# Attention mixed with a token MLP on one core: an eviction moved from ScalarE to VectorE, the start of a unit's maximum held back before some stretches, and one output store issued later

## The chip, the cores and the metric

The kernel runs on one core of a Trainium2 chip. The metric is the device time of one execution in microseconds (us); lower is better. The time before is the median of three runs, 1621.32 us (1620.71 to 1622.15). The core has five engines that are named here as the profile names them: PE is TensorE (PEld its weight loads), DVE is VectorE, ACT is ScalarE, POOL is GpSimd, and SP is the engine that issues nearly all DMAs. Each engine takes its instructions in the order in which the program lists them.

## The reference

The input is `x` with 2048 tokens of 640 channels. Two branches are computed from it and mixed with a gate of its own for each token. Branch A is attention with 32 query heads of 20 channels over one shared key head and one shared value head; branch B is an MLP across the tokens.

```python
g = _sigmoid((x * gate_w).sum(-1, keepdims=True))
# branch A
q = (x @ wq).reshape(B, S, H, Dh).transpose(0, 2, 1, 3)      # H = 32, Dh = 20
k, v = x @ wk, x @ wv                                        # one head for all queries
p = _softmax(jnp.einsum("bhqd,bkd->bhqk", q, k) * (Dh ** -0.5), axis=-1)
a = jnp.einsum("bhqk,bkd->bhqd", p, v).transpose(0, 2, 1, 3).reshape(B, S, H * Dh) @ wo
# branch B
h = _layernorm(x, axis=-1)
u = _gelu(jnp.einsum("bsd,sf->bdf", h, w1) + b1)             # F = 1728
b = jnp.einsum("bdf,fs->bds", u, w2) + b2                    # then transposed to (B, S, D)
return g * a + (1 - g) * b
```

## The kernel before, in words

**Units.** Attention is cut into 32 units: a unit is four heads by 512 queries. A unit needs three kinds of matrix work on PE. *Maxima*: scores of 128 queries by 512 keys are written to a bank of PSUM (`ms_next`, L506) and VectorE takes the maximum along the keys (L514, tile `mp`); 64 such tiles make a unit. The 64 partial maxima are put together by one VectorE reduction (`ms_done`, L536), three small POOL instructions (L532 to L534), a VectorE transpose (`store_max`, L541), a DMA to DRAM (`m_scr`, L542) and four DMAs that bring them back as two rows of the query tile (`fetch_max`, L549), so that the maximum is subtracted inside the score product itself. *Scores*: transposed scores of 128 keys by 512 queries (`qk`, L689), on which ScalarE computes the exponential (L701, tile `p`). *Values*: `p` times `v` (`pv_mm`, L722), four heads at once, which also sums the softmax denominators.

**Stretches and bursts.** The main loop runs 244 stretches, numbered `j`. `arrange` interleaves in one stretch eight score tiles, four to ten maxima tiles and some products of other work (`fs`) on the two row halves of PE, which run beside each other. After each stretch comes a burst: sixteen L722 matmuls (two key blocks of one unit). Its result is copied out by ScalarE (`collect`, L740 or L743) and added up by POOL (L744). The other work comes in three stages: products with W1 (L1012, 24 in each half and stretch), products with W2 (L837, 20, 20, 20 and then 21), and in the last 44 stretches the output projection of 11 token tiles (L961, 15 in each half and stretch). After the loop come 12 tail stretches (`stretch(i)`) with the remaining projections (L910), and then the end of the last unit.

**The planner.** Which instruction stands where is decided while the program is built: `begins`, `issue`, `spend` and `next_free` keep estimated clocks for the two PE lanes, for `dve` and `act`, and for each PSUM bank (`free`), and the next free bank and the next lane are taken by these clocks. On the chip each engine just follows its list and waits on semaphores. `end` in `arrange` is the list of functions that close a piece of other work; they are called when the last product of a stretch has been listed, right behind `signal()`, a tiny VectorE memset (`flag`, L711) that waits for that product and lets the other row half go on.

**The projection's end.** One projection (one token tile, half the channels) takes two stretches and accumulates in the bank `g`. `a_jobs.done` closes it. Before, the list `spare` holds False for the whole loop, so the else branch is always taken in it: ScalarE scales the sums by the gate (L972), POOL adds the MLP's part `yt` (L973). The store of the tile (L975) is appended to `stores` and issued a stretch later.

**The last maxima.** Unit 31's maxima are finished inside tail stretch 2; `m_scr` is written and fetched at its end, and tail stretch 4 is the first whose scores need them. The first tail projection (`jobs[0]`, token tile 11, tile `parts[st]`) is finished by VectorE (L922) in the same stretch 2, and its store (L926) is issued where it is finished, in front of the write of `m_scr` on SP's list.

Of the kernel before, what the change touches and what calls it, by code (L numbers as in the profile page):

```python
# [10 lines left out]
F32 = mybir.dt.float32  # L11
# [7 lines left out]
P = 128  # L19
# [20 lines left out]
def mix_kernel(ctx: ExitStack, tc: tile.TileContext, A_x, A_wq, A_wk, A_wv, A_wo,  # L40
# [635 lines left out]

    units = [(n, kb) for n in range(NU) for kb in range(NS)]
    ptiles = {}
    spare = [False]
    last = {"half": None, "ins": None, "sig": None}  # L680
    flag = const.tile([1, 1], F32, name="flag")

# [182 lines left out]
        nc.sync.dma_start(out=yt, in_=y_scr[st * P:(st + 1) * P, :])  # L865

    parts = {}
    tail = [[], []]
    loaded = []
    CUT = 3 * P  # L870
# [24 lines left out]
    def tail_job(n):  # L895
        st, r0, r1 = jobs[n]
        oT, yt = room(n)
        acc, at, ready = {}, {}, []

        def mm(c, k, d, h, first, last):  # L900
            if first:
                i = at[d, h] = busy[h] = next_free()
                while any(k == i for _, k, _ in reduces):
                    reduces.pop(0)[2]()
                acc[d, h] = bank(i)
                free[i] = float("inf")
            o, w = ((oT[:, 0], wo_hi), (oT[:, 1], wo_hi), (oT[:, 0], wo_lo))[k]
            r = slice(64 * h, min(r1 - c * P, 64 * h + 64))
            region = [("x", at[d, h])]
            touch(nc.tensor.matmul(acc[d, h][:, :HD2], o[r, c, :], w[r, c, d * HD2:(d + 1) * HD2],  # L910
                                   start=first, stop=last), writes=region)
            if last:
                ends = lane[h] + 0.15
                while reduces and reduces[0][0] < ends:
                    reduces.pop(0)[2]()
                free[at[d, h]] = spend("dve", 0.48, ends) + 0.24
                sl = slice(d * HD2, (d + 1) * HD2)
                if st not in parts:
                    parts[st] = fin.tile([P, D], F32, name="yo") if r1 == D else spare_row(st)
                add = parts[st] if d in ready or r0 else yt  # L920
                ready.append(d)
                touch(nc.vector.scalar_tensor_tensor(parts[st][:, sl], acc[d, h][:, :HD2], g_col[:, st:st + 1],  # L922
                                                     add[:, sl], op0=ALU.mult, op1=ALU.add), region)
                if len(ready) == 4:
                    if r1 - r0 == D:
                        nc.sync.dma_start(out=y_out[st * P:(st + 1) * P, :], in_=parts[st])  # L926
# [16 lines left out]
    def a_jobs(st):  # L943
        hold = {}

        def load():
            oT, yt = oTs[st % 2], yts[st % 2]
            load_a(st, D, oT, yt)
            hold["o"], hold["y"] = oT, yt
            hold["a"] = fin.tile([P, D], F32, name="yo")  # L950

        total = 6 * DC

        def mm(c, k, d, half):
            if not hold.get("n"):
                hold["p"], hold["n"] = ps_g.tile([P, NB], F32, name="g"), 0
            oT = hold["o"]
            o, w = ((oT[:, 0], wo_hi), (oT[:, 1], wo_hi), (oT[:, 0], wo_lo))[k]
            hold["n"] += 1
            r = slice(64 * half, 64 * half + 64)  # L960
            other_tile(half, nc.tensor.matmul(hold["p"][:, :HD2], o[r, c, :], w[r, c, d * HD2:(d + 1) * HD2],  # L961
                             start=(hold["n"] == 1), stop=(hold["n"] == total)))

        def done(d):
            sl = slice(d * HD2, (d + 1) * HD2)
            at, yt = hold["a"], hold["y"]
            hold["n"] = 0
            if spare[0]:
                nc.vector.scalar_tensor_tensor(at[:, sl], hold["p"][:, :HD2], g_col[:, st:st + 1], yt[:, sl],
                                               op0=ALU.mult, op1=ALU.add)  # L970
            else:
                nc.scalar.activation(at[:, sl], hold["p"][:, :HD2], AF.Copy, scale=g_col[:, st:st + 1])  # L972
                nc.gpsimd.tensor_add(at[:, sl], at[:, sl], yt[:, sl])  # L973
# [183 lines left out]
    def arrange(h, ss, own, other, fs, end):  # L1157
        ss, own, other, fs = list(ss), list(own), list(other), list(fs)
        n_s, n_m, n_f = len(ss), len(own), len(fs)
        lx, lf = layout(n_s, n_m, n_f, len(other))  # L1160
        pairs.clear()
        at = lx.replace("m", "").find("S")
        if at >= 0:
            pairs.update({at: 0, at + 1: 2})
        lx = [(k, (own if k == "m" else ss).pop(0)) for k in lx]
        lf = [(k, (other if k == "m" else fs).pop(0)) for k in lf]
        lanes = [None, None]
        lanes[h], lanes[1 - h] = lx, lf
        left = n_f
        while lanes[0] or lanes[1]:  # L1170
            k = min((k for k in range(2) if lanes[k]), key=lambda k: begins(k, lanes[k][0][0]))
            kind, f = lanes[k].pop(0)
            issue(k, kind, f)
            left -= kind == "f"
            if kind == "f" and not left:
                seen = lane[k] + 0.3
                while reduces and reduces[0][0] < seen:
                    reduces.pop(0)[2]()
                signal()
                spend("dve", 0.01)  # L1180
                state["f"] = seen + 0.6
                for f in end:
                    f()
                    state["f"] = max(state["f"], spend("act", 0.4, lane[k] + 0.2) + 0.1)
        while reduces:
            reduces.pop(0)[2]()

# [37 lines left out]
    for j in range(n_st):  # L1225
# [22 lines left out]
            f()  # L1248
        if follow:
            follow.pop(0)()  # L1250
        if not follow:
            n = len(row_max)
            follow += ms_done()
            if follow:
                follow.pop(0)()
                follow.append(lambda n=n: store_max(n))
# [19 lines left out]
    free.append(state["f"])  # L1276
    free[o_bank] = float("inf")
    o_last = {}
    spare[0] = True

    def visits(us):
        for u in us:
# [57 lines left out]
    def stretch(i):  # L1340
        u0 = 2 * n_st + 2 * i
        lanes, tiles = [None, None], [None, None]
        state["f"] = 0.0
        for b in range(2):
            block = []
            ss = [("s", lambda at, u=u, pr=pr, b=b, block=block: qk(u, pr, b, at, block))
                  for u in (u0, u0 + 1) for pr in range(2)]
            ms = [("m", ms_next(b)) for _ in range((3, 3, 2)[i] if i < 3 else 0)]
            lanes[b] = tail_take(b, math.ceil(len(tail[b]) / (TAIL // 2 - i)))
            tiles[b] = ms + ss if i == 2 else [x for n in range(4) for x in ss[n:n + 1] + ms[n:n + 1]]  # L1350
        for k in best_order(tiles, lanes, i):
            issue(k % 2, *(tiles, lanes)[k // 2][k % 2].pop(0))
        while reduces:
            reduces.pop(0)[2]()
        while stores:
            stores.pop(0)()
        if i == 2:
            for f in ms_done():
                f()
            store_max(NU - 1)  # L1360
            stores.pop()()
            fetch_max(NU - 1)
        settle()
# [12 lines left out]
    def next_acc():  # L1376
# [1 line left out]
        free[i] = max(free) + 1.0  # L1378
        return i

    assert not tail[0] and not tail[1] and not any(later)
    pool = pools["last"]
    whole = (pool.tile([P, NB // 32, 32], F32, name="ot"), pool.tile([P, NB // 32], F32, name="rl"),
             copies.tile([P, NB], F32, name="part"), *(pools["q5"][:, i, :] for i in range(2)))
    turn = [last_half(k, o_last[NU - 1], whole) for k in range(2)]
    for f in turn[0][:5] + turn[1][:2] + turn[0][5:] + turn[1][2:5]:
        f()
    accs = {}
# [73 lines left out]
```

## Time and profile before

| what | value |
|---|---|
| median of three runs | 1621.32 us |
| the profiled execution | 1621.41 us, of which the span from first to last instruction is 1619.6 us |
| busy, share of the span | PE 99%, VectorE 85%, ScalarE 78%, POOL 53% |
| instructions | 39588 |
| granted clock of TensorE | 1.00 |
| chain that ended last | PE 97% |
| L972, ScalarE, scale of a projection | 22 times, mean 612 ns |
| L973, POOL, its addition | 22 times, mean 878 ns |

The span and the execution's own time differ by 1.8 us, which lies around the instructions. A busy time in the profile runs from an instruction's start to its end; instructions of ScalarE and VectorE overlap by a part of that, so how fast they follow one another is read from the distance of their starts. PE counts as busy nearly throughout, even where its instructions wait for a bank, so a stretch is measured here from the start of one burst (L722) to the start of the next.

### The profile page before, as it was taken

Reading aid. Unit: us, or ns where it says so; the run is one execution under the profiler, and the core shown is the slowest. Engines: PE = TensorE matmul, PEld = TensorE weight load, DVE = VectorE, ACT = ScalarE, POOL = GpSimd, SP = SyncE. Lnnn points to the kernel's source line nnn. Section 1 sums busy time; section 2 is a strip of 40 time slices with the busy share of each in tenths; the row PEclk is TensorE's granted clock in tenths of the full one; section 3 lists DMA queues with packets and bytes.
Section 4 is the critical chain, followed back from the end, with each engine's and each line's share of the span. In section 5 each row is a group of like instructions: output and inputs, shape, how many; then the busy total and the mean of one; then the engine's idle time right before and its main releaser. Section 6 shows DMA issues by size and latency. Waiting matters only on the chain.

```text
span 1619.6 us, 39588 instructions
## 1 busy us (share of the span) xinstructions
PE 1611.0 (99%) x14868; PEld 1125.4 (69%) x14868; DVE 1374.8 (85%) x2607; ACT 1267.7 (78%) x2372; POOL 860.0 (53%) x949
## 2 busy tenths in 40 slices
PE   9999999999999999999999999999999999999998
PEld 7899876676677676666666666666666666666665
DVE  6689899999999999888888888888888885556653
ACT  4445677777777788888888888788887889999976
POOL 6567766777777776554455434444444423443421
PEclk9999999999999999999999999999999999999999
DMA  7655323222222222222211111112222113343221
GB/s 214 206 169 142 88 65 73 63 75 72 65 75 69 58 72 71 66 68 69 68 57 59 41 51 54 58 53 60 61 60 60 41 52 104 95 120 94 81 86 59
DMA packets 180309, 129.28 MB, mean 80 GB/s; under 512 B 41585, under 2 KB 150030, under 8 KB 180118
## 3 DMA queue, kind: packets, MB, share of 16 engines
q1 hardware_dynamic: 179830, 126.43, 27.8%
q8 instruction: 117, 1.92, 0.5%
q14 instruction: 74, 0.61, 0.1%
q10 hardware_dynamic: 288, 0.33, 0.1%
HBM read 93.57 MB, written 32.15 MB: 78 GB/s over the span
## 4 chain that ended last, share of the span: by engine, by line
PE 97%; SPq 1%; DVE 1%; DMA 0%; POOL 0%; issue 0%; ACT 0%; POOLq 0%; DVEq 0%
PE xs L722 29%; PE xs L689 18%; PE xs L506 18%; PE g L837 10%; PE g L1012 7%; PE pu L633 4%; PE pp L302 4%; PE g L961 3%; PE xs L910 1%; PE x L506 1%; PE pt L294 0%; PE xs L1427 0%; DVE st L235 0%; SPq L199 0%; DMA m_scr<-mt 0%
## 5 line engine op out<-in xcount | busy, mean ns | idle before, releaser
L514 DVE TENSOR_REDUCE mp<-xs 128x1 f32<-128x512 f32 x1946 | 1199.6, 683 | 167.9 <-PE xs L689 90.0
L701 ACT ACTIVATE p<-xs 128x512 f32<-128x512 f32 (+1 forms) x1829 | 1014.1, 687 | 9.8 <-PE xs L689 6.3
L744 POOL TENSOR_TENSOR osum<-osum,part 128x512 f32<-128x512 f32 x212 | 274.2, 1293 | 531.9 <-ACT part L743 527.0
L722 PE MATMUL xs<-p,v_sb 128*32 128x512 f32 x4096 | 492.3, 598 | 0.0
L689 PE MATMUL xs<-q,kst 62*128 62x512 f32 x1338 | 477.2, 418 | 1.3 <-ACT p L701 1.3
L506 PE MATMUL xs<-kst,q 60*128 60x512 f32 x1242 | 438.8, 417 | 0.0
L689 PEld LDWEIGHTS xs<-q,kst 62*128 62x128 f32 x1338 | 236.0, 185 | 74.8 <-DVE mp L514 51.5
L743 ACT ACTIVATE part<-xs 128x512 f32<-128x512 f32 x212 | 127.7, 602 | 196.6 <-PE xs L722 195.6
L1012 PE MATMUL g<-slot,w 64*128 64x320 f32 x1728 | 266.8, 306 | 0.0
L722 PEld LDWEIGHTS xs<-p,v_sb 128*32 128x32 f32 x4096 | 107.2, 109 | 224.9 <-issue 163.3
L506 PEld LDWEIGHTS xs<-kst,q 60*128 60x128 f32 x1242 | 209.8, 185 | 73.6 <-DVE mp L514 44.4
L1012 PEld LDWEIGHTS g<-slot,w 64*128 64x128 f32 x1728 | 259.2, 185 | 1.9
L127 POOL TENSOR_TENSOR w<-wr,w 128x512 fp32r<-128x512 f32 (+1 forms) x180 | 225.6, 1256 | 34.4 <-ACT w L124 20.8
L689 PE MATMUL xs<-slot,kst 62*128 62x512 f32 x563 | 206.6, 419 | 1.0 <-DMA slot<-m_scr 0.8
L506 PE MATMUL xs<-kst,slot 60*128 60x512 f32 x576 | 206.8, 419 | 0.0
L837 PE MATMUL g<-u,w 64*128 64x320 f32 x1296 | 201.7, 306 | 0.0
L837 PE MATMUL g<-slot,w 64*128 64x320 f32 x1296 | 201.4, 306 | 0.0
L837 PEld LDWEIGHTS g<-u,w 64*128 64x128 f32 x1296 | 195.7, 184 | 1.8
L837 PEld LDWEIGHTS g<-slot,w 64*128 64x128 f32 x1296 | 195.6, 184 | 1.6
L689 PEld LDWEIGHTS xs<-slot,kst 62*128 62x128 f32 x563 | 99.3, 185 | 33.8 <-DVE mp L514 22.6
L506 PEld LDWEIGHTS xs<-kst,slot 60*128 60x128 f32 x576 | 96.3, 185 | 33.8 <-DVE mp L514 21.2
L961 PE MATMUL g<-slot 64*128 64x320 f32 x660 | 107.7, 308 | 0.0
(198 smaller groups left out, 1502.0 us busy)
## 6 DMA issues: line engine op xcount, KB each, us to landing
wr<-in_B_w_dram SPq DMA_DIRECT2D x155, 256.0 KB
q<-q_scr SPq DMA_DIRECT2D x126, 80.0 KB
rb<-r_scr SPq DMA_DIRECT2D x120, 64.0 KB
slot<-o_scr SPq DMA_DIRECT2D x22, 320.0 KB
y_scr<-yo SPq DMA_DIRECT2D x16, 320.0 KB
q_scr<-qh SPq DMA_DIRECT2D x19, 256.0 KB
q_scr<-ql SPq DMA_DIRECT2D x19, 256.0 KB
o_scr<-rb SPq DMA_DIRECT2D x120, 40.0 KB
```

The costliest lines, as they stand in the source:

```text
L127: nc.gpsimd.tensor_sub(wl, wr, f32(wh))
L302: nc.tensor.matmul(pp, w, t, start=first and n == 0, stop=not more and n == len(steps) - 1)
L506: mm = nc.tensor.matmul(ms, qtiles[n][64 * b:64 * b + 60, pr, qt * P:(qt + 1) * P], kst[64 * b:64 * b + 60, kq * NB:(kq + 1) * NB], start= ...
L514: red = nc.vector.tensor_reduce(out, ms, axis=AX.X, op=ALU.max)
L689: mm = nc.tensor.matmul(s, kst[64 * b:64 * b + 62, kb * P:(kb + 1) * P], q[64 * b:64 * b + 62, pr, :], start=True, stop=True)
L701: act = nc.scalar.activation(p_all[:, a * NB:(j + 1) * NB], s, AF.Exp, scale=SCALE)
L722: mm = nc.tensor.matmul(o[32 * hh:32 * hh + 32, :], v_sb[:, units[u][1], :], p_all[:, j * NB:(j + 1) * NB], start=first, stop=last, skip_g ...
L743: touch(nc.scalar.activation(part, o, AF.Copy), [("x", i)])
L744: nc.gpsimd.tensor_add(osum[n], osum[n], part)
L837: other_tile(half, nc.tensor.matmul(hold["p"][:, :HD2], w[r, fc % HS, :], u[d][r, fc, :], start=(hold["n"] == 1), stop=(hold["n"] == 6 * F ...
L961: other_tile(half, nc.tensor.matmul(hold["p"][:, :HD2], o[r, c, :], w[r, c, d * HD2:(d + 1) * HD2], start=(hold["n"] == 1), stop=(hold["n" ...
L1012: other_tile(half, nc.tensor.matmul(hold["p"][:, :HD2], w[r, st % HS, :], h[d][r, st, :], start=(hold["n"] == 1), stop=(hold["n"] == 6 * NS)))
```

## The change

Three edits, and one that follows from the first.

1. `a_jobs.done` always takes the VectorE form: one `scalar_tensor_tensor` reads the sums in PSUM, multiplies by the gate and adds `yt`. L972 and L973 are gone. `spare` is gone with them.
2. The planner books the end of a projection (15 products in a half) on its `dve` clock and no longer on `act`; for the two earlier stages nothing changes.
3. In the loop the reduction of a unit's finished maxima is not started in front of a stretch with exactly 20 products in its half.
4. The store of token tile 11 is put in a list `whole` and issued in the first tail stretch behind number 2, after the last `fetch_max`. (The tuple that was called `whole` is now called `kept`.)

```diff
@@ a tail_job's end
                 if len(ready) == 4:
                     if r1 - r0 == D:
-                        nc.sync.dma_start(out=y_out[st * P:(st + 1) * P, :], in_=parts[st])
+                        whole.append(lambda: nc.sync.dma_start(out=y_out[st * P:(st + 1) * P, :], in_=parts[st]))
@@ a_jobs.done
-            if spare[0]:
-                nc.vector.scalar_tensor_tensor(at[:, sl], hold["p"][:, :HD2], g_col[:, st:st + 1], yt[:, sl],
-                                               op0=ALU.mult, op1=ALU.add)
-            else:
-                nc.scalar.activation(at[:, sl], hold["p"][:, :HD2], AF.Copy, scale=g_col[:, st:st + 1])
-                nc.gpsimd.tensor_add(at[:, sl], at[:, sl], yt[:, sl])
+            nc.vector.scalar_tensor_tensor(at[:, sl], hold["p"][:, :HD2], g_col[:, st:st + 1], yt[:, sl],
+                                           op0=ALU.mult, op1=ALU.add)
@@ arrange
                 for f in end:
                     f()
-                    state["f"] = max(state["f"], spend("act", 0.4, lane[k] + 0.2) + 0.1)
+                    state["f"] = max(state["f"], spend("act" if n_f > 15 else "dve", 0.4, lane[k] + 0.2) + 0.1)
@@ the loop over stretches
-        if not follow:
+        if not follow and not (j + 1 < n_st and len(ph[j + 1][0]) == 20):
             n = len(row_max)
             follow += ms_done()
@@ stretch(i)
             store_max(NU - 1)
             stores.pop()()
             fetch_max(NU - 1)
+        if i > 2 and whole:
+            whole.pop()()
```

Three places in the lists. First ScalarE, at the end of the first projection (of many lines the number is one lower in the changed kernel; L701 and L700 are the exponentials, L740 and L739 the copy of a burst's result, `xs_2757` and `xs_2761` the PSUM tiles of three and four banks). Before:

```order
L701 ACTIVATE p<-xs_2761 128x512 x2
L701 ACTIVATE p<-xs_2757 128x512
L701 ACTIVATE p<-xs_2761 128x512
L972 ACTIVATE yo<-g,g_col 128x320
L701 ACTIVATE p<-xs_2757 128x512
L740 ACTIVATE osum<-xs_2757 128x512
```

And now:

```order
L700 ACTIVATE p<-xs_2761 128x512 x2
L700 ACTIVATE p<-xs_2757 128x512
L700 ACTIVATE p<-xs_2761 128x512
L700 ACTIVATE p<-xs_2757 128x512
L739 ACTIVATE osum<-xs_2757 128x512
```

The copy out of the projection's bank has left ScalarE's list between two exponentials. At the same place VectorE's list now reads (L514 are the maxima, L710 is the memset behind a stretch's last product):

```order
L514 TENSOR_REDUCE mp<-xs_2761 128x1
L710 MEMSET flag 1x1
L968 SCALAR_TENSOR_TENSOR yo<-g,g_col,slot_80 128x320
L514 TENSOR_REDUCE mp<-xs_2761 128x1 x2
L514 TENSOR_REDUCE mp<-xs_2757 128x1 x2
L710 MEMSET flag 1x1
```

The new instruction stands right behind the memset and in front of the four maxima of the next stretch. Ahead of this place all five lists hold the same instructions in the same order as before. All stretches with 20 products lie ahead of it, so edit 3 moves nothing.

Second, PE at the last products of stretch `j` = 226, the first stretch with five maxima tiles (L961 are the projection's products, L689 and L688 scores, L506 maxima). Before:

```order
L506 MATMUL xs_2761<-kst,q 128x512
L506 MATMUL xs_2757<-kst,q 128x512
L961 MATMUL g<-slot_80 128x320 x3
L689 MATMUL xs_2761<-q,kst 128x512
L961 MATMUL g<-slot_80 128x320
L689 MATMUL xs_2757<-q,kst 128x512
```

And now:

```order
L506 MATMUL xs_2757<-kst,q 128x512
L506 MATMUL xs_2761<-kst,q 128x512
L961 MATMUL g<-slot_80 128x320 x2
L688 MATMUL xs_2761<-q,kst 128x512
L961 MATMUL g<-slot_80 128x320
L688 MATMUL xs_2757<-q,kst 128x512
L961 MATMUL g<-slot_80 128x320
```

One product has moved behind the last score. In all other stretches the kinds of matmuls stand in the same order as before, and only the banks that they are given differ.

Third, SP in the tail (L764 and L763 store the inverse sums of unit 30, L542 and L549 write and fetch the last maxima, L734 and L733 store unit 30's output, L926 is the store of token tile 11). Before:

```order
L764 DMA r_scr<-ls 128x16
L768 DMA rb<-r_scr 32x512 x4
L926 DMA out_dram<-yo 128x640
L542 DMA m_scr<-mt 128x32
L549 DMA slot_79<-m_scr 1x32x32 x4
L734 DMA o_scr<-rb 20x512 x4
L734 DMA o_scr<-osum 20x512 x4
```

And now:

```order
L763 DMA r_scr<-ls 128x16
L767 DMA rb<-r_scr 32x512 x4
L542 DMA m_scr<-mt 128x32
L549 DMA slot_79<-m_scr 1x32x32 x4
L733 DMA o_scr<-rb 20x512 x4
L733 DMA o_scr<-osum 20x512 x4
L926 DMA out_dram<-yo 128x640
```

The store has moved behind the write and the fetch of the last maxima and behind eight small stores.

More of the change, by code (lines that the diff above doesn't have):

```diff
@@ L678, in mix_kernel @@
     ptiles = {}
-    spare = [False]
     last = {"half": None, "ins": None, "sig": None}
@@ L867, in mix_kernel @@
     parts = {}
+    whole = []
     tail = [[], []]
@@ L1278, in mix_kernel @@
     o_last = {}
-    spare[0] = True
     def visits(us):
@@ L1379, in next_acc @@
         return i
-    assert not tail[0] and not tail[1] and not any(later)
+    assert not tail[0] and not tail[1] and not any(later) and not whole
     pool = pools["last"]
-    whole = (pool.tile([P, NB // 32, 32], F32, name="ot"), pool.tile([P, NB // 32], F32, name="rl"),
+    kept = (pool.tile([P, NB // 32, 32], F32, name="ot"), pool.tile([P, NB // 32], F32, name="rl"),
              copies.tile([P, NB], F32, name="part"), *(pools["q5"][:, i, :] for i in range(2)))
-    turn = [last_half(k, o_last[NU - 1], whole) for k in range(2)]
+    turn = [last_half(k, o_last[NU - 1], kept) for k in range(2)]
     for f in turn[0][:5] + turn[1][:2] + turn[0][5:] + turn[1][2:5]:
```

## The prediction

> **What bounds the kernel now.** I read the page first, and then the projection stage stretch by stretch. From the page: the span, the busy times and the chain that ended last.
>
> ```profile
> span 1619.6 us, 39588 instructions
> PE 1611.0 (99%) x14868; PEld 1125.4 (69%) x14868; DVE 1374.8 (85%) x2607; ACT 1267.7 (78%) x2372; POOL 860.0 (53%) x949
> PE 97%; SPq 1%; DVE 1%; DMA 0%; POOL 0%; issue 0%; ACT 0%; POOLq 0%; DVEq 0%
> ```
>
> PE is on the path all the way, so only what shortens a stretch on PE counts. The timeline of PE gives the lengths: the starts of the bursts around stretches 200 to 203, then from 226 on (first column, us).
>
> ```profile
> 1331.85 1.92 PE L722 MATMUL xs<-p,v_sb 128*32 128x512 f32 x16
> 1336.44 1.92 PE L722 MATMUL xs<-p,v_sb 128*32 128x512 f32 x16
> 1341.08 1.93 PE L722 MATMUL xs<-p,v_sb 128*32 128x512 f32 x16
> 1345.86 1.92 PE L722 MATMUL xs<-p,v_sb 128*32 128x512 f32 x16
> 1350.49 1.07 PE L722 MATMUL xs<-p,v_sb 128*32 128x512 f32 x8
> ...
> 1454.36 1.92 PE L722 MATMUL xs<-p,v_sb 128*32 128x512 f32 x16
> 1459.39 1.93 PE L722 MATMUL xs<-p,v_sb 128*32 128x512 f32 x16
> 1464.23 1.92 PE L722 MATMUL xs<-p,v_sb 128*32 128x512 f32 x16
> ```
>
> Stretch 200 takes 1336.44 - 1331.85 = 4.59 us, 201 takes 4.64, 202 takes 4.78, 203 takes 4.63. A projection ends at every odd stretch from 201 on; the even stretch behind it is the long one. Stretch 200 has the same kinds of matmul in the same order as 202, but no projection ends ahead of it. So 0.19 us of 202 is not PE's own work. The timeline of ScalarE for two later stretches of this kind (207 and 208, bursts at 1364.69, 1369.32 and 1374.12) says whose it is:
>
> ```profile
> 1366.74 0.60 ACT L743 ACTIVATE part<-xs 128x512 f32<-128x512 f32 x1
> 1367.24 3.53 ACT L701 ACTIVATE p<-xs 128x512 f32<-128x512 f32 x7
> 1370.58 0.61 ACT L972 ACTIVATE yo<-g,g_col 128x320 f32<-128x320 f32 x1
> 1370.98 0.69 ACT L701 ACTIVATE p<-xs 128x512 f32<-128x512 f32 x1
> 1371.46 0.70 ACT L743 ACTIVATE part<-xs 128x512 f32<-128x512 f32 x1
> 1371.94 4.14 ACT L701 ACTIVATE p<-xs 128x512 f32<-128x512 f32 x8
> 1376.17 0.60 ACT L743 ACTIVATE part<-xs 128x512 f32<-128x512 f32 x1
> ```
>
> Start to start, seven exponentials take 1370.58 - 1367.24 = 3.34 us, 0.477 each; L743 takes 0.50 and L972 takes 0.40. Two stretches need 16 x 0.477 + 2 x 0.50 + 0.40 = 9.03 us of the 1376.17 - 1366.74 = 9.43 that they last. L743 can't begin before its burst is done, and here the exponentials ahead of it run past that point: with L972 in between, the second L743 starts 1371.46 - 1369.32 = 2.14 us behind its burst's start, the first 1366.74 - 1364.69 = 2.05. From there the exponentials come late, and with them the banks that PE wants. ScalarE, not PE, sets this pair's length, by little.
>
> **Edits 1 and 2: the eviction.** They remove 22 ScalarE and 22 POOL instructions:
>
> ```profile
> L973 POOL TENSOR_TENSOR yo<-yo,slot 128x320 f32<-128x320 f32 x22 | 19.3, 878 | 59.4 <-ACT yo L972 59.4
> L972 ACT ACTIVATE yo<-g,g_col 128x320 f32<-128x320 f32 x22 | 13.5, 612 | 0.0
> ```
>
> ScalarE's two stretches then need 8.63 us against 2 x 4.61 = 9.22 of PE (4.61 lies between the 4.59 of stretch 200 and the 4.63 of 203). What is late next is PE itself. From 1341.08 to 1454.36 lie the 24 stretches 202 to 225: 113.28 us now, 24 x 4.61 = 110.64 then, 2.64 less. If only the twelve behind an end fall, from 4.78 to 4.61, it is 2.04. I take 2.3, between the two, since a part of the total may be other delays. Stretch 226 takes 1459.39 - 1454.36 = 5.03; with its last product behind the last score it has the order of 228 and should take the 4.84 of 227: 0.2 less, at worst nothing. Stretches 227 to 243 have five maxima tiles and take 4.84 whether an end lies ahead or not; ScalarE's 9.03 fits into 9.68 with 0.65 to spare, so I give them nothing.
>
> On VectorE the new instruction is of the kind of L922, which the trace has in the tail; its start and the next one's:
>
> ```profile
> 1557.36 0.55 DVE L922 SCALAR_TENSOR_TENSOR yo<-g,g_col,u 128x320 f32<-128x320 f32 x1
> 1557.82 1.28 DVE L514 TENSOR_REDUCE mp<-xs 128x1 f32<-128x512 f32 x2
> ```
>
> That is 0.46 us each, 22 x 0.46 = 10.1 us in all. The cover is the hole in VectorE's timeline behind the memset, with four maxima tiles and with five:
>
> ```profile
> 1364.82 0.06 DVE L711 MEMSET flag<- 1x1 f32 x1
> 1367.09 2.56 DVE L514 TENSOR_REDUCE mp<-xs 128x1 f32<-128x512 f32 x4 [2.08 <-PE xs L689]
> ...
> 1474.52 0.06 DVE L711 MEMSET flag<- 1x1 f32 x1
> 1476.31 3.21 DVE L514 TENSOR_REDUCE mp<-xs 128x1 f32<-128x512 f32 x5 [1.73 <-PE xs L506]
> ```
>
> VectorE waits 2.08 and 1.73 us there for the next stretch's first maxima, during the burst. The memset has already waited for the projection's last product, so the new instruction waits for nothing on PE; the row `yt` was needed by POOL at the same place. Behind it are queued the next maxima, for whose banks PE waits, and the bank `g`, which PE wants only behind the burst. I cost it at nothing; without the cover it would be up to 10.1. POOL's 19.3 us are off the path: nothing, either way. The stores of the tiles (L975) wait for VectorE now and no longer for POOL, and nobody waits for them.
>
> The Trainium skill, Perfetto Trace Analysis, section Optimizing Scalar/DVE Operations, speaks against moving a read of PSUM this way: it gives a fixed cost of about 125 ns for VectorE on PSUM and about 51 ns for ScalarE. The rows agree in direction, 0.46 against 0.40 us. If those 74 ns lay on the path 22 times, my estimate by that page would be 1.6 us less gain, some 1619.6 us; by the rows they lie in the hole.
>
> **Edit 3** moves no instruction in any list, since every unit's maxima already ended ahead of a 21-product stretch there: zero, from both sides.
>
> **Edit 4: the store.** SP's timeline around it, a small write of the same way through DRAM elsewhere (L764 to L768), and PE at the place that waits:
>
> ```profile
> 1429.10 0.38 SPq L764 DMA_DIRECT2D r_scr<-ls  x1
> 1431.03 1.25 SPq L768 DMA_DIRECT2D rb<-r_scr  x3
> ...
> 1559.59 0.36 SPq L926 DMA_DIRECT2D out_dram<-yo  x1
> 1560.88 0.34 SPq L542 DMA_DIRECT2D m_scr<-mt  x1
> 1563.93 2.75 SPq L549 DMA_DIRECT2D slot<-m_scr  x4
> ...
> 1364.69 1.92 PE L722 MATMUL xs<-p,v_sb 128*32 128x512 f32 x16
> 1366.55 0.50 PE L506 MATMUL xs<-kst,q 60*128 60x512 f32 x1
> ...
> 1564.13 1.92 PE L722 MATMUL xs<-p,v_sb 128*32 128x512 f32 x16
> 1566.88 0.47 PE L689 MATMUL xs<-slot,kst 62*128 62x512 f32 x1 [0.83 <-DMA slot<-m_scr]
> ```
>
> The issue of the store ends at 1559.95, before the write of the maxima is due, so SP's list is not what is held. But the write takes 3.05 us until the fetch can be issued, the other small write 1.93: the store's 320 KB are in flight ahead of it. Without them the fetch starts at about 1560.88 + 1.93 = 1562.81 and PE's rows are there 2.95 us later as now, at 1565.76. PE restarts 1.86 us behind a burst's start, here at 1565.99: the whole wait goes, 1566.88 - 1565.99 = 0.89. Bounds are 0 and 0.89; I take 0.85. The store now stands behind four fetches and eight small stores; behind it are stores of unit 30's output, and its 0.36 us of issue lie in time that SP waits. Nothing.
>
> **The sum.** 2.3 + 0.2 + 0.85 = 3.35 us from the profiled execution's 1621.41 gives 1618.06. That execution lies 0.09 above the median of the runs, so 1618.0. About 0.2% (3.2 us) is what a measurement of this kernel can tell from no change; the line lies at 1618.1, within the spread of my terms.
>
> **Rivals.**
> - *The long stretch is not ScalarE's doing*, but that of the products waiting for `g` behind an end. Then edits 1 and 2 give nothing and the store's 0.85 is left: 1620.5. Against it: L743 late by 0.09 just there.
> - *The last write is slow without the store as well.* For it: one small write of the same kind is all that I compare with. Then 2.5 is left: 1618.8.
> - *The five-maxima stretches fall too.* A fifth tile costs 4.84 - 4.61 = 0.23, and the timeline of PE has scores at this distance,
>
> ```profile
> 1371.75 0.39 PE L689 MATMUL xs<-slot,kst 62*128 62x512 f32 x1
> 1371.98 0.39 PE L689 MATMUL xs<-slot,kst 62*128 62x512 f32 x1
> ```
>
>  0.23 apart. Two row halves could share it at 0.12: 17 x 0.11 = 1.9 more, 1616.1. Against it: their order is unchanged.
> - *VectorE comes late, and the kernel is slower.* At each of the 22 ends the new instruction pushes the next maxima back by 0.46, and PE waits as long for their banks: 10.1 - 3.35 = 6.7 more, 1628.1. It decides from the point where the hole is under 0.46; it is 1.73 or more. The planner has handed out banks anew by its own clocks, which could bring such a wait where none was.
>
> **How the numbers follow.** The forecast holds with 0.65; its terms (2.04 to 2.64, 0 to 0.2, 0.8 to 0.89) span 1617.6 to 1618.5, of which I count 0.45 beyond the line and 0.20 short of it. The first rival has 0.11, the second 0.12, the third 0.06, the slower one 0.06. Faster by over 0.2%: 0.45 + 0.06 = 0.51; within: 0.20 + 0.11 + 0.12 = 0.43; slower: 0.06. The range 1616.9 to 1620.6 takes in the forecast and the first two rivals and leaves out the others.
>
> **What would show it.** Right: even stretches 202 to 224 of 4.59 to 4.64 us; L743 at 2.05 us behind every burst; the new instruction of 0.55 us inside the hole; no PE wait on the fetched maxima; about 1.9 us between L542 and L549. Wrong: long stretches that stay, a VectorE wait ahead of PE's first maxima, or a fetch that is still issued 3 us behind its write.

## The result, and the profile after

The changed kernel takes 1618.49 us (median of 19 runs, 1618.04 to 1619.48), the one before 1621.51 (median of 19 runs beside it, 1620.71 to 1622.26). The ratio is 0.9981, 95% interval 0.9974 to 0.9988: 3.0 us faster, near the line that the prediction drew for what can be measured. The forecast was 1618.0 us in a range of 1616.9 to 1620.6.

The page of the profile after, in the same three rows:

```profile
span 1616.5 us, 39520 instructions
PE 1608.8 (100%) x14868; PEld 1123.3 (69%) x14868; DVE 1383.9 (86%) x2629; ACT 1261.1 (78%) x2350; POOL 841.1 (52%) x927
PE 98%; POOL 0%; DVE 0%; DMA 0%; issue 0%; ACT 0%; POOLq 0%; SPq 0%; DVEq 0%
```

PE is on the path as before, and the span is 3.1 us shorter. Lines behind L680 of the file have moved up: L722 is now L721, L743 is L742, L701 is L700, L689 is L688, and the new VectorE instruction is L968. The starts of PE's bursts, from the timeline (stretches 201 to 204, then from 226 on):

```profile
1336.52 1.92 PE L721 MATMUL xs<-p,v_sb 128*32 128x512 f32 x16
1341.14 1.92 PE L721 MATMUL xs<-p,v_sb 128*32 128x512 f32 x16
1345.77 1.92 PE L721 MATMUL xs<-p,v_sb 128*32 128x512 f32 x16
1350.40 1.92 PE L721 MATMUL xs<-p,v_sb 128*32 128x512 f32 x16
...
1452.08 1.92 PE L721 MATMUL xs<-p,v_sb 128*32 128x512 f32 x16
1456.92 1.92 PE L721 MATMUL xs<-p,v_sb 128*32 128x512 f32 x16
1461.76 1.92 PE L721 MATMUL xs<-p,v_sb 128*32 128x512 f32 x16
```

Stretch 202 takes 1345.77 - 1341.14 = 4.63 us as its neighbours do (4.78 before), the 24 stretches from 202 to 225 take 1452.08 - 1341.14 = 110.94 (113.28 before), stretch 226 takes 4.84 (5.03 before). ScalarE at the place where L972 stood:

```profile
1357.56 4.02 ACT L700 ACTIVATE p<-xs 128x512 f32<-128x512 f32 x8
1361.70 0.60 ACT L742 ACTIVATE part<-xs 128x512 f32<-128x512 f32 x1
1362.19 4.02 ACT L700 ACTIVATE p<-xs 128x512 f32<-128x512 f32 x8
1366.29 0.60 ACT L742 ACTIVATE part<-xs 128x512 f32<-128x512 f32 x1
1366.79 4.02 ACT L700 ACTIVATE p<-xs 128x512 f32<-128x512 f32 x8
```

The bursts of the two L742 (PE's timeline):

```profile
1359.62 1.92 PE L721 MATMUL xs<-p,v_sb 128*32 128x512 f32 x16
1364.24 1.92 PE L721 MATMUL xs<-p,v_sb 128*32 128x512 f32 x16
```

L742 starts 2.08 and 2.05 us behind them. Eight exponentials start to start are 8 x 0.477 = 3.82 us, so ScalarE has 1361.70 - 1357.56 - 3.82 = 0.32 and 1366.29 - 1362.19 - 3.82 = 0.28 us to spare ahead of each L742. VectorE around an end and the stretch behind it (start, us, what; the last bracket is the idle time before it and what ended it):

```profile
1359.89 0.55 DVE L968 SCALAR_TENSOR_TENSOR yo<-g,g_col,slot 128x320 f32<-128x320 f32 x1
1359.90 0.06 DVE L710 MEMSET flag<- 1x1 f32 x1
1362.05 2.52 DVE L514 TENSOR_REDUCE mp<-xs 128x1 f32<-128x512 f32 x4 [1.61 <-PE xs L506]
```

The new instruction lies in the hole, and 1.61 us of the hole are left behind it. At last SP's queue and PE at the last fetch:

```profile
1558.34 0.34 SPq L542 DMA_DIRECT2D m_scr<-mt  x1
1560.87 2.75 SPq L549 DMA_DIRECT2D slot<-m_scr  x4
...
1566.78 0.36 SPq L926 DMA_DIRECT2D out_dram<-yo  x1
```

```profile
1561.59 1.92 PE L721 MATMUL xs<-p,v_sb 128*32 128x512 f32 x16
1563.69 0.47 PE L688 MATMUL xs<-slot,kst 62*128 62x512 f32 x1 [0.18 <-DMA slot<-m_scr]
```

The store stands behind the fetches. The interval from write to fetch is 2.53 us: shorter than 3.05, longer than the 1.93 of the forecast. PE still waits 0.18 of its 0.83 us.

The same lengths for every kernel of the study, worked out from the starts of the bursts in PE's timeline (us; "even" and "odd" are means over the twelve stretches of 202 to 225 each; "wait" is the stretch with the fetched maxima; "time" is the median against that of the kernel before on the same chip, with the 95% interval of the ratio; each length comes from the one profiled execution of its kernel):

```
kernel                24 str.  even  odd   226   227-243 wait  time  ratio
before                113.28   4.80  4.64  5.03   82.11  5.91
after                 110.93   4.62  4.62  4.84   82.06  5.26  -3.0  0.9974-0.9988
e1 edits 1 to 3       111.00   4.63  4.62  4.85   82.10  5.78  -2.6  0.9976-0.9993
e2 edit 4             113.29   4.80  4.64  5.02   82.11  5.09  -0.7  0.9987-1.0004
e3 edit 1             111.39   4.66  4.62  4.84   82.06  5.48  -2.5  0.9976-0.9994
e4 edit 2             112.97   4.80  4.61  5.03   82.40  5.22  -0.1  0.9991-1.0008
e5 after, 1 ACT copy  112.22   4.73  4.62  4.95   82.26  5.02  -1.7  0.9982-1.0000
e6 after, 3 on DVE    110.93   4.62  4.62  4.85   83.66  5.44  -1.4  0.9983-1.0001
e7 after, 6 on DVE    129.64   6.18  4.62  6.41  102.24  5.66 +39.5  1.0234-1.0262
e8 two stores         110.91   4.62  4.62  4.85   82.08  6.66  -1.9  0.9981-0.9999
e9 after, PE shifted  110.99   4.63  4.62  4.85   82.11  5.01  -2.5  0.9975-0.9993
e10 e1, PE shifted    110.98   4.63  4.62  4.85   82.09  5.02  -2.4  0.9976-0.9993
e11 after, 2 copies   118.06   5.22  4.62  5.45   85.44  5.13  +7.9  1.0036-1.0061
```

After against before: 2.35 us from the 24 stretches, 0.19 from 226, 0.65 from the wait, 3.19 in all; the first burst starts 0.2 later (189.05 against 188.84), which varies between 188.4 and 189.3 over kernels that are alike up to there.

### The profile page after: what moved, and what is told of

Read it like the earlier page. It is cut to its first block, busy times and chain, and to the rows that moved or that the text cites. A ratio compares the mean times of both kernels' runs of the same rounds, so it can differ in the third digit from the quotient of the medians.

```text
span 1616.5 us, 39520 instructions
## 1 busy us (share of the span) xinstructions
PE 1608.8 (100%) x14868; PEld 1123.3 (69%) x14868; DVE 1383.9 (86%) x2629; ACT 1261.1 (78%) x2350; POOL 841.1 (52%) x927
## 3 DMA queue, kind: packets, MB, share of 16 engines
q8 instruction: 117, 1.92, 0.5%
## 4 chain that ended last, share of the span: by engine, by line
PE 98%; POOL 0%; DVE 0%; DMA 0%; issue 0%; ACT 0%; POOLq 0%; SPq 0%; DVEq 0%
PE xs L721 29%; PE xs L688 18%; PE xs L506 18%; PE g L836 11%; PE g L1008 7%; PE pp L302 4%; PE pu L633 4%; PE g L961 3%; PE xs L910 1%; PE x L506 1%; PE pt L294 0%; PE pp L366 0%; PE xs L1424 0%; PE pp L191 0%; PE g L688 0%
## 5 line engine op out<-in xcount | busy, mean ns | idle before, releaser
L514 DVE TENSOR_REDUCE mp<-xs 128x1 f32<-128x512 f32 x1943 | 1196.9, 684 | 154.7 <-PE xs L688 78.4
L700 ACT ACTIVATE p<-xs 128x512 f32<-128x512 f32 (+1 forms) x1834 | 1011.7, 680 | 10.9 <-PE xs L688 6.4
L743 POOL TENSOR_TENSOR osum<-osum,part 128x512 f32<-128x512 f32 x212 | 274.2, 1294 | 604.8 <-ACT part L742 597.9
L721 PE MATMUL xs<-p,v_sb 128*32 128x512 f32 x4096 | 492.3, 598 | 0.0
L688 PE MATMUL xs<-q,kst 62*128 62x512 f32 x1339 | 476.2, 417 | 1.3 <-ACT p L700 1.3
L506 PE MATMUL xs<-kst,q 60*128 60x512 f32 x1242 | 437.4, 416 | 0.0
L688 PEld LDWEIGHTS xs<-q,kst 62*128 62x128 f32 x1339 | 235.9, 185 | 74.6 <-DVE mp L514 52.3
L742 ACT ACTIVATE part<-xs 128x512 f32<-128x512 f32 x212 | 126.8, 598 | 199.6 <-PE xs L721 197.3
L721 PEld LDWEIGHTS xs<-p,v_sb 128*32 128x32 f32 x4096 | 106.9, 109 | 225.5 <-issue 161.0
L506 PEld LDWEIGHTS xs<-kst,q 60*128 60x128 f32 x1242 | 209.6, 184 | 73.4 <-DVE mp L514 44.4
L688 PE MATMUL xs<-slot,kst 62*128 62x512 f32 x567 | 206.9, 418 | 0.4 <-DVE row L922 0.2
L506 PE MATMUL xs<-kst,slot 60*128 60x512 f32 x573 | 205.3, 418 | 0.0
L688 PEld LDWEIGHTS xs<-slot,kst 62*128 62x128 f32 x567 | 99.7, 185 | 31.7 <-DVE mp L514 22.6
L506 PEld LDWEIGHTS xs<-kst,slot 60*128 60x128 f32 x573 | 96.2, 184 | 33.1 <-DVE mp L514 20.4
L961 PE MATMUL g<-slot 64*128 64x320 f32 x660 | 106.7, 306 | 0.0
```

What stands on the lines that cost most here:

```text
L506: mm = nc.tensor.matmul(ms, qtiles[n][64 * b:64 * b + 60, pr, qt * P:(qt + 1) * P], kst[64 * b:64 * b + 60, kq * NB:(kq + 1) * NB], start= ...
L514: red = nc.vector.tensor_reduce(out, ms, axis=AX.X, op=ALU.max)
L688: mm = nc.tensor.matmul(s, kst[64 * b:64 * b + 62, kb * P:(kb + 1) * P], q[64 * b:64 * b + 62, pr, :], start=True, stop=True)
L700: act = nc.scalar.activation(p_all[:, a * NB:(j + 1) * NB], s, AF.Exp, scale=SCALE)
L721: mm = nc.tensor.matmul(o[32 * hh:32 * hh + 32, :], v_sb[:, units[u][1], :], p_all[:, j * NB:(j + 1) * NB], start=first, stop=last, skip_g ...
L742: touch(nc.scalar.activation(part, o, AF.Copy), [("x", i)])
```

## The experiments: which edit brings what

**e1, edits 1 to 3 without the store.** The store goes back to its old place:

```
-  whole.append(lambda: nc.sync.dma_start(out=y_out[...], in_=parts[st]))
+  nc.sync.dma_start(out=y_out[...], in_=parts[st])
```

> Edits 1 to 3 without edit 4: the eviction on VectorE as in the changed kernel, the store of token tile 11 at its old place. Theory (ScalarE set the length of the long stretches): 24 stretches 202 to 225 about 111.0 us instead of 113.3, stretch 226 4.84 instead of 5.03, the write of the maxima again 3.05 us ahead of its fetch, PE's wait there 0.8; 2.4 to 2.6 us less than before. Rival (the gain came from the moved store and from chance): the stretches fall no further than 113, 0 to 0.3 us less.

Measured: the 24 stretches take 111.00, stretch 226 4.85, from the write of the maxima to its fetch are 3.07, PE waits 0.7 there, and the time is 2.6 us less. The theory holds.

**e2, edit 4 alone**: the kernel before with its store behind the last fetch (the lines of the change on `whole`).

> Edit 4 alone, everything else as before. Theory: the fetch is issued about 2.5 us behind the write instead of 3.05, the tail's stretch is 0.65 us shorter, the 24 stretches stay at 113.3; 0.5 to 0.7 us less than before. By the prediction's own term it would be 0.85 less with the interval at 1.93. Rival (the write is as slow without the store): 3.0 us between write and fetch, no change.

Measured: the long stretches are as before, the interval from write to fetch is 2.36, PE does not wait, and the median is 0.7 us less, an amount that its interval can't tell from none. By the stretch of the wait it is 0.82.

**e3, the eviction alone, and e4, the planner's booking alone.** In e3 `if spare[0]:` becomes `if True:` in the kernel before, and nothing else changes; in e4 only the booking does:

```
-  state["f"] = max(state["f"], spend("act", 0.4, lane[k] + 0.2) + 0.1)
+  state["f"] = max(state["f"], spend("act" if n_f > 15 else "dve", 0.4, lane[k] + 0.2) + 0.1)
```

> Edit 1 alone: the eviction is one VectorE instruction, but the planner still books it on ScalarE, so that the list of PE and all banks are those of before. Theory (ScalarE's 0.40 us per end was what the long stretches waited for, wherever the banks lie): 24 stretches at 110.9 to 111.3, 2.0 to 2.5 us less than before. Rival (the new hand-out of banks did it, or is needed for it): 24 stretches above 112.5, under 0.8 us less, and PE waiting for VectorE's maxima behind an end.

> Edit 2 alone: the planner books the eviction on VectorE and hands out the banks as in the changed kernel, but ScalarE and POOL still do the work. Theory (ScalarE): ScalarE has as much to do as before, the 24 stretches stay at 113.0 to 113.6, within 0.4 us of before either way. Rival (banks): 24 stretches at 111 to 112, 1.5 to 2.4 us less.

The starts of stretches 202, 226 and 227 in PE's timeline of e3, then of e4:

```profile
1340.55 1.92 PE L722 MATMUL xs<-p,v_sb 128*32 128x512 f32 x16
1451.95 1.92 PE L722 MATMUL xs<-p,v_sb 128*32 128x512 f32 x16
1456.79 1.92 PE L722 MATMUL xs<-p,v_sb 128*32 128x512 f32 x16
```

```profile
1341.31 1.50 PE L722 MATMUL xs<-p,v_sb 128*32 128x512 f32 x12
1454.28 1.92 PE L722 MATMUL xs<-p,v_sb 128*32 128x512 f32 x16
1459.31 1.92 PE L722 MATMUL xs<-p,v_sb 128*32 128x512 f32 x16
```

The 24 stretches take 111.40 in e3, a little more than the 110.9 to 111.3 expected, and 112.97 in e4, a little less than the 113.0 to 113.6, where 113.28 stood. Edit 1 brings 1.9 us of them without new banks; edit 2 brings 0.3 in the odd stretches and loses as much in 227 to 243. Together they give 0.4 to 0.5 more than edit 1 alone. So where the work is done decides most of it; the banks add a little, and only where the work has moved.

Stretch 226 takes 4.84 in e3 and 5.03 in e4. PE's list in e3 is that of the kernel before, with the last product ahead of the last score; in e4 it is that of the changed kernel. So the 0.19 of this stretch comes from ScalarE as well, and not from the product that moved.

## The experiments: what ScalarE and VectorE can bear

**e5 and e11, ScalarE's time put back.** One (e5) or two (e11) copies on ScalarE behind the new instruction, which still frees `g` at once:

```
   nc.vector.scalar_tensor_tensor(at[:, sl], ..., op1=ALU.add)
+  nc.scalar.activation(at[:, sl], at[:, sl], AF.Copy, scale=1.0)     # e11: twice
```

> The changed kernel, and at each of the 22 ends ScalarE also copies the new half row of `yo` in place (128x320, about as long as the removed eviction). VectorE still frees the bank `g` at once. Theory (ScalarE's time): the even stretches 202 to 224 are back at 4.75 to 4.80 us, 226 at 5.0, 2.0 to 2.6 us more than the changed kernel, about 1620.6. Rival (the products waited for the bank `g` to be read, the prediction's first): since VectorE reads it as early as before, the stretches stay at 4.62 and the time at 1618.5.

> As the run with one copy on ScalarE at each end, now two. Theory (ScalarE sets the length of the even stretches): each further copy of 0.36 us adds as much, so 5.0 to 5.1 us for the even stretches 202 to 224 instead of 4.73, 4 to 5 us more than with one copy, and the stretches with five maxima begin to grow too. Rival (the 0.10 us of one copy was a fixed price of another kind): 4.73 to 4.80.

ScalarE's timeline at such a copy in e5, then in e11; the next row's start less its own is the time that it takes from the exponentials:

```profile
1370.37 0.54 ACT L969 ACTIVATE yo<-yo 128x320 f32<-128x320 f32 x1
1370.73 0.67 ACT L700 ACTIVATE p<-xs 128x512 f32<-128x512 f32 x1
```

```profile
1371.49 1.05 ACT L969 ACTIVATE yo<-yo 128x320 f32<-128x320 f32 x2
1372.45 0.58 ACT L700 ACTIVATE p<-xs 128x512 f32<-128x512 f32 x1
```

ScalarE gives 0, 0.36 and 0.96 us per end, and the even stretches take 4.62, 4.73 and 5.22; with the 0.40 of L972 before the change it was 4.80. The odd stretches stay at 4.62. So the long stretch follows ScalarE's time, 0.49 for 0.60 between one and two copies, and the rival of the bank `g` falls: it was free as early as in the changed kernel. A sum for the stretch alone gives the lengths: eight exponentials and L742 are 3.82 + 0.50 = 4.32 us, and with the work at the end 4.68 (one copy), 4.72 (L972) and 5.28 (two copies), all over PE's 4.62; measured were 4.73, 4.80 and 5.22. Both runs missed their numbers: one copy cost 1.3 us in time and not 2.0 to 2.6, two cost 9.7 more than one and not 4 to 5, since the second added 0.60 instead of 0.36 and the stretches from 227 on grew too (85.44). Why L972 cost 0.07 more than the copy, which is 0.04 shorter, stays open.

**e6 and e7, VectorE's cover.** `for _ in range(3):` (e7: 6) ahead of the new instruction, so that it is issued three or six times with the same result.

> The changed kernel with the new VectorE instruction issued three times at each end, each with the same result: 0.92 us more on VectorE at 22 places. Theory (the hole hides it; about 1.6 us of it are left behind one instruction where four maxima follow, some 1.3 where five do): no change, within 0.4 us of 1618.5. Rival (every VectorE instruction there pushes the maxima and PE back): up to 22 x 0.92 = 20 us more.

> As the run with three, now six times at each end: 2.30 us more on VectorE at 22 places, which is more than the 1.6 and 1.3 us that are left. Theory (a hole of that size): each end costs PE up to 0.7 us (four maxima) or 1.0 us (five), 8 to 18 us more than the changed kernel. Rival (the banks ahead of PE hold more slack than the hole shows): under 3 us more. In either case VectorE's idle time ahead of the next maxima is gone behind an end.

With three, the stretches with four maxima do not move (110.93), but those with five grow by 0.2 at each of eight ends (83.66), 1.6 us where I expected none. With six, every stretch behind an end grows, 42 us where I expected 8 to 18. Two rows of PE, one with four maxima and one with five, show what waits:

```profile
1366.85 0.41 PE L961 MATMUL g<-slot 64*128 64x320 f32 x1 [1.20 <-DVE yo L968]
...
1511.18 0.41 PE L961 MATMUL g<-slot 64*128 64x320 f32 x1 [1.56 <-DVE yo L968]
```

The waits of e7, summed (us in total, times, longest):

```profile
PEld g L961 <- DVE yo L968: 37.3, 21, 2.0
PE g L961 <- DVE yo L968: 28.2, 21, 1.6
```

PE waits for `g`, which the last of the six instructions still reads, not for the maxima. VectorE's rows of e7 at the first of these places give the price of one:

```profile
1363.31 0.55 DVE L968 SCALAR_TENSOR_TENSOR yo<-g,g_col,slot 128x320 f32<-128x320 f32 x1
1363.33 0.06 DVE L710 MEMSET flag<- 1x1 f32 x1
1363.89 2.90 DVE L968 SCALAR_TENSOR_TENSOR yo<-g,g_col,slot 128x320 f32<-128x320 f32 x5
```

Start to start the copies are 0.58 apart, where L922 had given 0.46 to a maximum behind it. They write the same tile and read the same bank; which of the two spaces them is not shown. The new instruction starts 0.27 us behind its burst in the changed kernel (1359.89, burst 1359.62), and PE wants `g` 2.19 us behind a burst, as e6 shows in a stretch without an end ahead of it:

```profile
1486.03 1.93 PE L721 MATMUL xs<-p,v_sb 128*32 128x512 f32 x16
...
1488.22 0.31 PE L961 MATMUL g<-slot 64*128 64x320 f32 x1
```

With 0.57 each, three are done at 0.27 + 1.72 = 1.99, in time; six at 0.27 + 3.45 = 3.72, 1.53 too late, and the stretch grew by 1.56. In a stretch with five maxima VectorE comes later to the instruction, as e6's rows of VectorE and PE show:

```profile
1491.48 0.55 DVE L968 SCALAR_TENSOR_TENSOR yo<-g,g_col,slot 128x320 f32<-128x320 f32 x1
1491.50 0.06 DVE L710 MEMSET flag<- 1x1 f32 x1
1492.06 1.14 DVE L968 SCALAR_TENSOR_TENSOR yo<-g,g_col,slot 128x320 f32<-128x320 f32 x2
```

```profile
1490.86 1.93 PE L721 MATMUL xs<-p,v_sb 128*32 128x512 f32 x16
...
1493.26 0.41 PE L961 MATMUL g<-slot 64*128 64x320 f32 x1
```

It starts 0.62 behind the burst, ends three at 2.34, and PE's first product stands at 2.40 instead of 2.19: the 0.2 of those stretches. The product starts 0.06 behind the end of the third there. So with one instruction, which takes 0.55, some 1.3 and 1.0 us are left to spare, an estimate from these rows; the 1.2 us more of e6 stayed hidden in the one case and not in the other.

## The experiments: the last write

**e8, two stores ahead of the write.** As e1, and behind the store a second one of the same tile into `y_scr`, which nobody reads any more.

> The changed kernel with the store of token tile 11 at its old place, and behind it the same 320 KB once more into the scratch `y_scr`, both ahead of the small write of the maxima. Theory (the write is late by what is in flight ahead of it): the interval from the write to its fetch grows from 3.07 to 3.6 to 4.2 us and PE's wait from 0.7 to 1.2 to 1.9, 1 us more than with one store. Rival (the write is late by something else, and one store more or less does little): 2.4 to 3.1 us, as in the runs so far with and without the store.

```profile
1557.19 0.36 SPq L926 DMA_DIRECT2D out_dram<-yo  x1
1557.59 0.43 SPq L926 DMA_DIRECT2D y_scr<-yo  x1
1558.48 0.32 SPq L542 DMA_DIRECT2D m_scr<-mt  x1
1562.32 2.74 SPq L549 DMA_DIRECT2D slot<-m_scr  x4
```

```profile
1565.23 0.47 PE L688 MATMUL xs<-slot,kst 62*128 62x512 f32 x1 [1.57 <-DMA slot<-m_scr]
```

3.84 us and a wait of 1.57, as the theory had it. But the interval also varied between kernels with the same traffic: with one store 3.05 (before), 3.07 (e1), 2.71 (e3) and 2.52 (e4), without one 2.53 (after), 2.36 (e2), 2.29 (e5), 2.76 (e6), 2.88 (e7) and 2.41 (e11). So a second thing acts on it.

The trace's records of single DMA packets show it. Times are us from the issue of the write; its 128 rows of 128 bytes go over 16 engines. "Code" is a 16384-byte packet of the queue that the page lists as `q8 instruction: 117, 1.92, 0.5%`: 117 packets, one for 256 of PE's some 30,000 instructions (2 x 14868 and its waits), 12 to 16 us apart here.

```
kernel   store ahead  code packet     rows done: 93%  last   fetch issued
before   320 KB       -0.25 to 1.20              1.40  2.46   3.05
e4       320 KB       -0.32 to 0.81              1.55  1.87   2.52
e2       none         -0.20 to 1.14              1.29  1.50   2.36
e1       320 KB        1.03 to 1.96              1.06  2.12   3.07
e3       320 KB        0.64 to 1.62              1.06  1.78   2.71
after    none          0.43 to 1.42              1.06  1.58   2.53
e8       640 KB        1.65 to 2.62              1.50  3.25   3.84
e9       none         -1.47 to -0.50             1.02  1.06   1.43
e10      320 KB       -1.58 to -0.61             1.01  1.06   1.46
```

In all but the last two kernels a last group of eight rows, one sixteenth of the write, comes late. In `after`, e1 and e3 it ends 0.16 us behind the code packet, with the store ahead or without it. In `before` and e4 the packet lies ahead of the store's own last eight rows: the other 120 rows of the store are there by 0.54, these eight end at 2.38 and 1.79, and the last eight rows of the write stand 0.08 behind them. That reads as one engine held by the packet, together with what the store had put on that engine. (In `before`, e2 and e4 an 8192-byte packet of another queue, `q14 instruction`, holds eight rows more; it ends at 1.32, 1.42 and 1.48, and in e2 the rows behind it are the last.) In e8 the store's part shows by itself: the first row is there at 1.25 instead of 0.84 or 0.85, 0.4 us later; the rest of its delay is again eight rows behind a code packet and two rows of the store.

The other writes of maxima in the traces agree. Each of the 13 kernels has 32 of them. Where a code packet lay on the time at which the rows come (0.85 to 1.06 us behind the issue), the last row was behind 1.10 us in all 34 cases, and in 31 of them it ended 0.11 to 0.17 us behind the packet. Where none lay there, the last row was in by 1.10 us in 334 of 382 cases; 39 of the other 48 are the same three writes of each kernel, with 227 to 655 packets of 256 bytes or more on the data queue within 1.5 us of the issue.

**e9 and e10, the code packet moved away.** PE's program is made 60 instructions longer at its very start, in e9 on the changed kernel, in e10 on e1:

```
-  for i in range(6):
-      nc.tensor.matmul(warm, kst[:, :P], kst[:, :NB], start=True, stop=True)
+  for i in range(36):
+      nc.tensor.matmul(warm[:4, :32], kst[:, :4], kst[:, :32], start=True, stop=True)
```

> The changed kernel; at its very beginning the six idle matmuls of 512 columns (L191) are replaced by 36 of 32 columns, so that everything PE issues later stands 60 instructions further on in its program; all orders stay. In the runs so far a 16384-byte packet of PE's instruction queue (one per some 256 PE instructions, 13.9 us apart here) lies on one DMA engine within 0.3 us before to 1.7 us behind the issue of the last write, and that engine delivers its rows of the write last. Theory (this packet holds the write): with the packet some 3 us earlier the interval from write to fetch falls from 2.53 to 1.9 to 2.1 us, no PE wait on the fetched maxima, 0.2 us less than the changed kernel at most. Rival (this write is slower than the other small one by itself): 2.3 to 2.9 us as before.

> The same 60 instructions more, with the store of token tile 11 at its old place ahead of the write. Theory (instruction packet and store share one DMA engine, and only together they cost 3.05 us): 1.9 to 2.2 us from write to fetch, no PE wait, as fast as the changed kernel, so that edit 4 is worth nothing here. Rival (the store alone holds the write): 2.5 to 3.1 us and a PE wait of 0.2 to 0.8.

SP and PE in e10, with the store ahead of the write:

```profile
1558.51 0.36 SPq L926 DMA_DIRECT2D out_dram<-yo  x1
1559.80 0.34 SPq L542 DMA_DIRECT2D m_scr<-mt  x1
1561.26 2.75 SPq L549 DMA_DIRECT2D slot<-m_scr  x4
```

```profile
1563.05 1.92 PE L721 MATMUL xs<-p,v_sb 128*32 128x512 f32 x16
1564.90 0.49 PE L688 MATMUL xs<-slot,kst 62*128 62x512 f32 x1
```

The packet moved by 2.6 us against e1 and, in e9, by 1.9 us against the changed kernel. The interval is 1.46 us with the store and 1.43 (e9) without, PE waits in neither, and the stretch of the wait is 5.02 and 5.01. That is the theory, and more than it expected (1.9 to 2.2). One 320 KB store ahead cost this write 0.03 us here, where no code packet falls on it. Of the 1.1 us by which e9 is shorter than the changed kernel, 0.52 are the last row. The rest lies between the last row and the fetch, 0.37 (e9) and 0.40 us (e10) here, and 0.59 to 0.96 in all others; what that part is stays open. In time e9 and e10 cannot be told from the changed kernel: -2.5 and -2.4 us against -3.0, with intervals of some 1.4 either way. So they are no faster version that could be shown.

## Why the prediction was right, and where not

- **ScalarE sets the long stretches: shown.** Forecast 2.3 (2.04 to 2.64), measured 2.35, of which 2.10 in the even stretches and 0.25 in the odd ones; L742 starts 2.05 to 2.08 behind its burst, and e3, e5 and e11 carry the cause. One step was soft: it weighed a pair of stretches, 9.03 us of 9.43, where ScalarE seems to have 0.40 to spare. The end loads only one of the two, whose own sum is 4.72 against PE's 4.62; the other's room, 0.3 us, is of no use to it.
- **Stretch 226**: 0.2 forecast, 0.19 measured, but for a reason that failed. The prediction gave the 0.2 to the product that moves behind the last score. With the old order and no work on ScalarE (e3) the stretch takes 4.84, with the new order and L972 still there (e4) 5.03, with copies on ScalarE 4.95 (e5) and 5.45 (e11): it is the thirteenth of the long stretches, and the number was right by luck. **Stretches 227 to 243**: nothing forecast, 0.05 measured; the third rival is out.
- **VectorE at nothing: right, for another reason than the one given.** The slower rival said that the maxima would be pushed back and that it decides where the hole is under 0.46. By e6 and e7 the bank `g` decides: the products want it 2.19 us behind the burst. I had named `g` and dismissed it in half a sentence. The size of the cover, some 1.3 and 1.0 us behind one instruction, came out near the hole's all the same. The sentence on the Trainium skill (Perfetto Trace Analysis, Optimizing Scalar/DVE Operations) had 74 ns more for VectorE's read at 22 ends; no part of it shows in the time, the odd stretches being 4.62 and the even ones 4.62.
- **Edit 3 at nothing**: it moves no instruction, and all stretches that it could touch lie ahead of 202. From the first burst to that of 202 are 1152.24 us before, 1152.09 after and 1152.03 in e3, which lacks it.
- **Edit 4 mis-sized, and its cause only half right: 0.85 forecast, 0.65 measured.** The step that failed is "the store's 320 KB are in flight ahead of it", taken as the whole delay, so that the fetch would start 1.93 behind the write. The write stayed at 2.53, between the forecast and the second rival (slow without the store as well), and PE still waits 0.18. The runs showed in its place a code packet of PE on one DMA engine, which makes the write late with the store and without it. What the store adds depends on where that packet lies. Where the packet comes ahead of the store's last rows, it is 0.69 (before against e2) or 0.16 (e4 against e2); where it comes behind them (e1, e3), the last row follows the packet as it does without a store; without a packet on the write it is 0.03 (e10 against e9). So the 0.65 is not shown to be the store's alone: e4, with the store in its old place, has 5.22 in the stretch of the wait and the changed kernel 5.26, and by edit 4 alone the stretch fell by 0.82 (e2 against before) and 0.52 (after against e1). That 0.65 came out near 0.85 is in part luck. Whether the store also moves the packet stays open. The Trainium skill (Runtime: NRT & Kernel Launch, Instruction fetch mechanics) says that an engine's program comes in blocks of 16 KiB, 256 instructions, over its own DMA queue, at a cost that is mostly hidden. The records agree with the block; no wait of PE for its own code shows in the traces, but the cost was not hidden for the small write in its way, which PE then waited for.
- **The sum**: 3.35 forecast. The terms measured 2.35 + 0.19 + 0.65 = 3.19 in the profiles, and the medians differ by 3.02. The 0.17 between them is less than the 0.9 by which the first burst's start scatters; where it lies is not shown. The median, 1618.49, lies between the forecast's 1618.0 and the second rival's 1618.8, and it is the rows of the last write that tell them apart.

## What to carry to other kernels

Look for stretches that repeat with small differences in length: an engine that is busy for less than a pair of them lasts can still set one of the two, and moving 0.4 us of its work into another engine's hole was worth 0.17 to 0.19 us at 13 of the 22 places, and next to nothing at the others, where the stretch is longer. When work is put into a hole, ask who wants the bank or buffer that it reads, not only what the engine does next. A small write that others wait for is as late as its slowest DMA engine, so compare it over several kernels before giving its delay to the transfer that is seen beside it.

## What was not expected of the hardware

- A packet of PE's own code, 16384 bytes and 0.92 to 1.45 us on one DMA engine, held the last rows of a 16 KB write until 1.36 (e5) to 1.92 us (e7) behind its issue instead of 1.06 (e9), without any store ahead; 60 instructions more at the start of PE's program took it away from there (1.43 us from write to fetch instead of 2.53).
- In e7, where PE waited 1.2 to 1.6 us at each end, the granted clock fell three times for some microseconds, all behind stretch 226; at the ends before, with waits of 1.2, it stayed at 1.00, and what brings the fall is not shown. Stretches 230, 238 and 240 took 8.20, 8.31 and 7.90 us where the other five behind an end took 6.77 or 6.78, and 241 took 5.25 instead of 4.83: an estimate of some 4.5 of the 39.5 us that is the clock and not the wait. The row of its windows (stretch and length, then busy time of PE, PEld, DVE, ACT and POOL, granted clock, DMA share, GB/s):

```profile
1496.00:1502.00 6.00, 4.43 (x28) 3.74 (x26) 4.64 (x9) 3.88 (x8) 2.51 (x2) 0.74 0.01 3
```

- Instructions that write the same tile one behind the other came 0.58 us apart on VectorE (e7) instead of 0.46, and 0.57 on ScalarE (e11) instead of 0.36.
